# Paired residue tails, slot sums from ScalarE, wide early slot outputs and a new order of stores in an attention and mixture-of-experts kernel

## The chip, the cores and the metric

The kernel runs on one core of a Trainium2 chip. The metric is the device time in microseconds (us) of that core. The six executions of the kernel before beside the changed one lie within 0.3% of their median (181.59 to 182.62 us around 182.07); some executions of other kernels are slower by more (order4: two of 185.53 and 187.42 us, two of 198.23 and 199.43) and are called slow. Each run lists the core's span and the mean granted clock of TensorE (1.0 is full speed; the clock records of the traces of before and after hold 1.0 and 0.5 alone). The median of the kernel before was 182.08 us (182.07 to 182.35) when the prediction was made.

## The reference, cut to what matters

```python
# attention: batch 8, heads 8, sequence 576, head size 64
# heads 0-3: rel = i - j in [0, 32)        (the "plain" heads)
# heads 4-7: rel in [0, 128), rel % 4 == 0 (the "dilated" heads)
x = softmax(mask(q @ k.T / 8)) @ v              # x: 4608 tokens x 512
# soft mixture of experts: 8 experts, 4 slots each, hidden size 1024
logits = x @ phi                                # 4608 x 32
d = softmax(logits, axis=0)                     # over the tokens, for each slot
slot_input = d.T @ x                            # 32 x 512
slot_out[e] = relu(slot_input[e] @ w1[e]) @ w2[e]
out = softmax(logits, axis=1) @ slot_out        # 4608 x 512
```

Nothing can be stored before all of the attention is done, because a slot sums over all tokens; and no output column before all of w1 and that column of every w2 have been read. The loads are converted from f32 to f16 on the way, the stores from f16 to f32 (on the page of the kernel before, 61.93 MB are read from HBM and 9.44 MB written).

## The kernel before

A dilated head is four interleaved sequences ("residues") of 144 tokens. A product of this kernel takes 128 of them (128*128 in the lines of the trace), so each residue leaves a tail of 16. These are the scores and the products with v as the kernel before has them:

```python
# scores, second group of a batch (g == 1): four narrow products a head for the tails
for r in range(DIL):                               # DIL = 4
    w = LEFT if r < 3 else 2 * LEFT                # LEFT = 16
    jobs.append((kd, SUB * r + 96, qd, SUB * r + 128, W1 + LEFT * r, w))
...
# emit_av, last group of the dilated heads: 128-column products, then the tails
elif t < DIL:
    jobs.append((0, 128, n, pt[:, h % 2, 128 * t : 128 * t + 128], vD[...]))
else:
    for r in range(DIL):                           # 48 rows x 32 columns of the array
        c0 = W1 + LEFT * r
        jobs.append((32 * r, 32, n, pt[0:48, h % 2, c0 : c0 + 32], vL[b % NV][0:48, h, r, 0 : D + 1]))
...
# back_u: slot inputs, and a product with ones that sums the exponentials
for c in range(2):
    jobs.append((c, x[:, c, :], er[0:n, t, :]))
jobs.append((4, ones[0:n, :], er[0:n, t, :]))
```

After the last batch it forms the slot outputs in two halves of 256 columns, and stores 16 of the 36 blocks of 128 tokens as left halves while the right halves of two experts are still loading.

The softmax here doesn't subtract the row's maximum and nothing guards it: scores larger than these inputs give would overflow.

## Time and profile before

| | before |
|---|---|
| median time | 182.08 us |
| profiled span, mean clock | 181.0 us, 0.868 |
| one batch of attention at full clock | 13.67 us |
| last slot-input product ends | 136.77 us |
| first store issued | 152.88 us |

Second, two batches late in the attention (windows of the same trace; the last three columns are granted clock, DMA share and GB/s).

```profile
84.87:98.54 13.67, 13.45 (x271) 8.52 (x270) 10.47 (x23) 9.19 (x16) 6.32 (x9) 1.00 1.17 209
98.54:112.21 13.67, 13.46 (x272) 8.51 (x271) 10.49 (x23) 9.19 (x16) 5.88 (x8) 1.00 1.16 210
```

A window here runs from the first bias product of a batch to that of the next. At full clock a batch is 13.67 us, and TensorE is busy for 13.45 of them: it is the engine that paces the attention.

### The profile page before, as it was taken

Reading aid. Unit: us, or ns where it says so; the run is one execution under the profiler, and the core shown is the slowest. Engines: PE = TensorE matmul, PEld = TensorE weight load, DVE = VectorE, ACT = ScalarE, POOL = GpSimd, SP = SyncE. Lnnn points to the kernel's source line nnn. Section 1 sums busy time; section 2 is a strip of 40 time slices with the busy share of each in tenths; the row PEclk is TensorE's granted clock in tenths of the full one; section 3 lists DMA queues with packets and bytes.
Section 4 is the critical chain, followed back from the end, with each engine's and each line's share of the span. In section 5 each row is a group of like instructions: output and inputs, shape, how many; then the busy total and the mean of one; then the engine's idle time right before and its main releaser. Section 6 shows DMA issues by size and latency. Waiting matters only on the chain.

```text
span 181.0 us, 5591 instructions
## 1 busy us (share of the span) xinstructions
PE 146.4 (81%) x2464; PEld 87.4 (48%) x2464; DVE 107.5 (59%) x232; ACT 91.0 (50%) x162; POOL 83.9 (46%) x124
## 2 busy tenths in 40 slices
PE   0467977999999999999999999999987986598000
PEld 0133544746755665664674674675735363233000
DVE  4689874875757676588498498453604023389030
ACT  2044454748465484755766776675430024488030
POOL 7953552642623263352544327434410442979900
PEclk9999995798589789789999999999855699879855
DMA  4999999999999999999999999999999999999996
GB/s 60 199 196 208 208 210 214 201 211 214 202 212 214 203 212 214 201 211 213 203 214 211 204 216 210 214 215 215 211 216 213 200 193 163 311 332 409 410 404 239
DMA packets 29527, 40.75 MB, mean 225 GB/s; under 512 B 1856, under 2 KB 19264, under 8 KB 29504
## 3 DMA queue, kind: packets, MB, share of 16 engines
q0 software_dynamic: 28960, 39.36, 116.3%
q1 hardware_dynamic: 544, 1.05, 1.5%
q8 instruction: 19, 0.31, 0.6%
q14 instruction: 4, 0.03, 0.0%
HBM read 61.93 MB, written 9.44 MB: 394 GB/s over the span
## 4 chain that ended last, share of the span: by engine, by line
DMA 43%; PE 34%; ACT 6%; DVE 6%; POOL 5%; issue 3%; POOLq 0%; DVEq 0%
DMA w<-in_moe_w_dram 28%; DMA raw<-in_k_dram 9%; ACT p L293 5%; PE lg L408 5%; PE o_p L339 4%; PE sa L282 4%; DMA out_dram<-ol 4%; PE sb L271 4%; PE sa L271 4%; DMA out_dram<-ot 2%; PE rd L389 2%; DVE qk L245 2%; PE vb L163 2%; PE va L163 2%; PE u L452 2%
## 5 line engine op out<-in xcount | busy, mean ns | idle before, releaser
L293 ACT ACTIVATE p<-sa 128x960 f16<-128x960 f32 (+2 forms) x24 | 21.4, 891 | 33.9 <-PE sb L282 33.4
L339 PEld LDWEIGHTS <-p 128*128 128x128 f16 (+2 forms) x544 | 19.7, 99 | 12.8 <-issue 8.6
L245 DVE STREAM_TRANSPOSE qk<-raw 128x320 uint32<-128x320 uint32 (+1 forms) x32 | 21.6, 678 | 0.3
L271 PE MATMUL sa<-masks,ident 128*128 128x480 f16 (+2 forms) x48 | 15.6, 414 | 7.3 <-POOL masks L489 6.2
L293 ACT ACTIVATE p<-sb 128x960 f16<-128x960 f32 (+2 forms) x24 | 21.2, 884 | 0.0
L236 DVE STREAM_TRANSPOSE qk<-raw 128x576 uint32<-128x576 uint32 x16 | 19.8, 1249 | 0.9 <-DMA raw<-in_q_dram 0.8
L271 PEld LDWEIGHTS <-ident 128*128 128x128 f16 x96 | 9.6, 112 | 18.9 <-issue 7.7
L282 PEld LDWEIGHTS <-qk 32*128 32x128 f16 x832 | 12.6, 100 | 12.0 <-issue 9.8
L408 PE MATMUL lg<-xTd,phi 128*128 128x288 f16 x32 | 18.3, 659 | 0.0
L339 PE MATMUL o_p<-v,p 128*128 128x65 f16 (+1 forms) x288 | 16.6, 202 | 0.8 <-ACT v L172 0.7
L282 PE MATMUL sa<-qk 32*128 32x160 f16 (+4 forms) x416 | 16.5, 217 | 0.8 <-DVE qk L236 0.7
L282 PE MATMUL sb<-qk 32*128 32x160 f16 (+4 forms) x416 | 16.5, 218 | 0.0
L271 PE MATMUL sb<-masks,ident 128*128 128x480 f16 (+2 forms) x48 | 15.4, 411 | 0.5 <-ACT p L293 0.5
L209 POOL COPY v<-v 32x1024 f16<-32x1024 f16 x8 | 8.3, 1036 | 16.1 <-PE sb L282 9.4
L212 POOL DMA_DIRECT2D w<-in_moe_w_dram x16 | 8.9, 554 | 14.4 <-DMA vs<-in_v_dram 6.8
L361 DVE TENSOR_TENSOR xp<-o_p,rc_p 128x448 f16<-128x448 f32 (+1 forms) x24 | 14.4, 602 | 0.8
L361 DVE TENSOR_TENSOR xd<-o_d,rc_d 128x448 f16<-128x448 f32 (+1 forms) x24 | 14.4, 602 | 0.8
L219 POOL DMA_DIRECT2D w<-in_moe_w_dram x10 | 6.7, 673 | 14.5 <-DMA w<-in_moe_w_dram 10.2
L163 PE MATMUL va<-vs,orders 32*128 32x256 f16 (+1 forms) x96 | 12.1, 289 | 1.0 <-ACT p L293 1.0
L412 ACT ACTIVATE ET<-lg 128x288 f16<-128x288 f32 x16 | 6.6, 411 | 12.3 <-PE lg L408 12.1
L360 DVE RECIPROCAL rc_p<-o_p 128x7 f32<-128x7 f32 (+1 forms) x24 | 4.8, 198 | 12.1 <-PE o_p L339 11.6
L382 ACT COPY xTp<-rp 128x576 f16<-128x576 f16 x16 | 10.4, 647 | 2.2 <-PE rp L377 2.2
(108 smaller groups left out, 277.9 us busy)
## 6 DMA issues: line engine op xcount, KB each, us to landing
w<-in_moe_w_dram POOLq DMA_DIRECT2D x16, 512.0 KB, 16.8
w<-in_moe_w_dram POOLq DMA_DIRECT2D x5, 1024.0 KB, 19.3
vs<-in_v_dram POOLq DMA_DIRECT2D x8, 512.0 KB, 14.5
raw<-in_q_dram POOLq DMA_DIRECT2D x7, 576.0 KB, 16.6
raw<-in_k_dram POOLq DMA_DIRECT2D x7, 576.0 KB, 16.8
out_dram<-ot POOLq DMA_DIRECT2D x14, 256.0 KB, 4.2
out_dram<-of POOLq DMA_DIRECT2D x7, 512.0 KB, 4.9
w<-in_moe_w_dram POOLq DMA_DIRECT2D x8, 256.0 KB, 10.2
```

What stands on the lines that cost most here:

```text
L163: nc.tensor.matmul(o.rearrange("p (h d) -> p h d", h=4), l, st[:, 0:4, D * r : D * r + D], start=(r == 0), stop=(r == DIL - 1), skip_group ...
L209: nc.gpsimd.tensor_copy(out=vL[b % NV][0:32, :, :, 0:D], in_=vD[b % NV][96:128, :, :, 0:D])
L212: nc.gpsimd.dma_start(out=w1t[e][:, 2 * i : 2 * i + 2, :].rearrange("p l f -> p (l f)"), in_=moe_w1[e, 256 * i : 256 * i + 256].rearrange( ...
L236: nc.vector.transpose(out=dst, in_=src)
L245: nc.vector.transpose(out=o, in_=i)
L271: nc.tensor.matmul(sps[h // 2][:, h % 2, 0:n], ident, bias[g], start=True, stop=False, skip_group_check=True,)
L282: nc.tensor.matmul(sps[h // 2][:, h % 2, c0 : c0 + w], kt_[32 * h : 32 * h + 32, k0 : k0 + 128, tt], qt_[32 * h : 32 * h + 32, q0 : q0 + w ...
L293: nc.scalar.activation(out=pt, in_=sps[ab][:, :, 0:n], func=AF.Exp, scale=SCALE)
L339: nc.tensor.matmul(o[p0 : p0 + np_, n, :], l, rr, start=(k == 0), stop=(k == len(jobs) - 1), skip_group_check=True,)
L361: nc.vector.tensor_tensor(out=x.rearrange("p t (h d) -> p (t h) d", h=4)[0:nq, u0:u1, :], in0=o[0:nq, 0:n, 0:D], in1=rc[0:nq, 0:n, None].b ...
L382: nc.scalar.copy(out=xTp_t[b][:, c, :], in_=rg)
L408: nc.tensor.matmul(lp, phi4[:, kc].rearrange("p c s -> p (c s)"), rhs, start=(kc == 0), stop=(kc == 3))
```

## The change

The intent: fewer and larger products for the tails (two residues in one), no products with ones, early slot outputs 512 columns wide, 20 left-half blocks instead of 16 to cover the last loads, stores four blocks at a time with four tokens a row, and rows of 4 KB. The core of the diff:

```diff
-NLEFT = 5 * LEFT
+NLEFT = DIL * LEFT
-NSPLIT = 16
+NSPLIT = 20
@@ emit_scores (the left keys are gathered by a new copy on VectorE)
-                for r in range(DIL):
-                    w = LEFT if r < 3 else 2 * LEFT
-                    jobs.append((kd, SUB * r + 96, qd, SUB * r + 128, W1 + LEFT * r, w))
+                for u in range(2):
+                    jobs.append((kL[b % 2], 128 * u, None, 0, W1 + NLEFT * u, NLEFT))
+                    if qt_ is None:
+                        qq = qd[heads, 0:S, tt].rearrange("p (r i) -> p i r", r=DIL)[:, 128:SUB]
@@ emit_av
-                for r in range(DIL):
-                    c0 = W1 + LEFT * r
-                    jobs.append((32 * r, 32, n, pt[0:48, ...], vL[b % NV][0:48, h, r, 0 : D + 1]))
+                for u in range(2):
+                    c1 = W1 + NLEFT * (u + 1)
+                    m = (128, 64)[u]
+                    jobs.append((128 - m, m, n, pt[:, h % 2, c1 - m : c1], vL[b % NV][:, h, u, 0 : D + 1]))
@@ back_xT_dil (fifth transpose)
+            p0 = 0 if r < DIL else NLEFT
+                xd_t[b][p0:128, r, 128 * c : 128 * c + 128], ident[p0:128, p0:128],
@@ back_logits, back_u
+            accum_out=esum[:, 2 * b + half : 2 * b + half + 1],
-            jobs.append((4, ones[0:n, :], er[0:n, t, :]))
@@ prologue, on VectorE before the first transposes of q and k
+        nc.vector.tensor_scalar(out=masks[:, W1:], in0=masks[:, W1:], scalar1=gap, scalar2=None, op0=ALU.max)
@@ weights, slot outputs, stores
+    LATE_ROWS = {MIXED: ((4, 8),), 6: ((0, 8),), 7: ((0, 4), (4, 8))}
+        slot_out(so_early, 0, early, True, True)
+        nc.scalar.copy(out=early_sb, in_=so_early)
+        return out[t0 : t0 + 512].rearrange("(p k) n -> p k n", k=4)[:, blk % 4 : blk % 4 + n]
... (allocations, masks, copies of v, order of the stores and buffers cut)
```

## The prediction

> **What bounds the kernel now.** I read the page first, for the shape of the whole span.
>
> ```profile
> PE   0467977999999999999999999999987986598000
> DMA  4999999999999999999999999999999999999996
> GB/s 60 199 196 208 208 210 214 201 211 214 202 212 214 203 212 214 201 211 213 203 214 211 204 216 210 214 215 215 211 216 213 200 193 163 311 332 409 410 404 239
> ```
>
> The DMA row is full from the first slice to the last. Loads halve their bytes on the way (f32 to f16), so 210 GB/s written is about 420 read; stores do the opposite and reach 409. The kernel is one DMA stream of 30.9 MB written by loads, then 9.44 MB of stores. What can be won is where the rate falls between (slices of 163, 311, 332), and what can be lost is a store that comes late. Next I cut that stretch into windows of 1 us (the last two columns are DMA share and GB/s).
>
> ```profile
> 151.00:152.00 1.00, 0.49 (x6) 0.38 (x6) 0.00 (x0) 0.37 (x1) 0.00 (x0) 1.00 1.40 188
> 152.00:153.00 1.00, 0.98 (x10) 0.72 (x9) 0.71 (x2) 0.82 (x2) 0.12 (x1) 1.00 0.93 125
> 153.00:154.00 1.00, 0.81 (x13) 0.28 (x10) 1.00 (x3) 1.00 (x4) 1.00 (x3) 1.00 0.73 107
> 154.00:155.00 1.00, 0.68 (x12) 0.40 (x5) 0.85 (x2) 0.73 (x3) 1.00 (x2) 1.00 1.37 246
> 160.00:161.00 1.00, 1.00 (x5) 0.49 (x4) 0.89 (x2) 0.88 (x3) 0.86 (x2) 0.80 0.70 136
> 166.00:167.00 1.00, 0.89 (x6) 0.38 (x4) 1.00 (x3) 1.00 (x3) 1.00 (x2) 1.00 1.52 406
> ```
>
> Two holes: 152 to 156, where some DMA engines have finished their share of the last loads and no store is queued, and 160 to 161, where the left-half stores are through and the first full-width store is not yet issued. By packet sizes, 0.28 MB of loads (1.4 us at 195 GB/s) and 2.47 MB of stores (6.0 us at 409) moved between 152 and 162: 7.5 us of work in 10, so 2.5 us were lost. The time line tells why.
>
> ```profile
> 146.54 3.38 PE L722 MATMUL so<-w,hTm 128*32 128x256 f16 x104 [0.38 <-DVE hTm L703]
> 151.04 0.29 PE L722 MATMUL so<-w,hTm 128*32 128x256 f16 x4 [1.11 <-DMA w<-in_moe_w_dram]
> 152.88 1.09 POOL L746 DMA_DIRECT2D out_dram<-oo  x2 [5.80 <-DVE oo L743]
> 153.96 5.01 POOL L784 DMA_DIRECT2D out_dram<-ot  x7
> 159.82 2.43 POOL L814 DMA_DIRECT2D out_dram<-of  x3 [0.84 <-ACT of L803]
> ```
>
> The last left half of w2 lands at 151.0, the first store is issued 1.9 us later and its packets flow from 154.0. Seven stores of 256 KB take 5.01 us to issue, 0.72 each, while the transfer needs 0.64: issue-bound. And TensorE waits for the left half only 1.11 us. That is all the slack the compute chain has; before it, TensorE is busy 13.46 of 13.67 us of a batch (window 96.00 to 109.67, clock 1.00).
>
> [...]
>
> ```profile
> 100.46 0.28 PE L422 MATMUL ep<-ident,ET 32*128 32x32 f16 x4
> 100.68 0.21 PE L428 MATMUL ep<-ident,ET 32*32 32x32 f16 x4
> 100.82 0.39 PE L339 MATMUL o_d<-v,p 128*128 128x65 f16 x7
> 101.04 0.52 PE L377 MATMUL rp<-ident,xp 128*128 128x128 f16 x5
> 103.08 0.47 PE L339 MATMUL o_d<-v,p 128*128 128x65 f16 x18
> 103.48 0.53 PE L377 MATMUL rp<-ident,xp 128*128 128x128 f16 x5
> ```
>
> Seven o_d matmuls of one mode take 0.22 us from start to start of the next group (0.03 each), but four transposes that start at 100.68 hold the next mode back until 100.82 though they start within 0.01 of each other. In every change of mode that I looked up in this batch the start-to-start time is 0.11 to 0.13 instead of 0.03: about 0.09 us a change. [...] of the logits' matmuls of 288 columns, those that read xTd with a stride occupy 18.3 us in 32, those that read xTp in order 7.2; start to start it is 0.48 against 0.125 us, 1.66 ns a column against 0.43. [...] here the fill rate is the same 405 to 413 for 1 KB and 2 KB store packets, so I expect nothing from rows of 4 KB.
>
> **The change, part by part.**
> 1. Stores. 20 blocks instead of 16 leave as left halves, so they cover 2.62 MB / 0.409 = 6.4 us instead of 5.1. By fours a store is 512 KB (1.28 us of transfer) for one issue; loads with four pieces per partition issue in 0.75, so the issue bound goes: about 0.35 us.
> 2. Loads. Right halves of 2.5 experts are 1.31 MB instead of 1.05: the last left half lands 1.3 us earlier, near 149.7. A quarter MB more on either side goes in 512-byte packets (197 GB/s instead of 214): +0.2 us.
> 3. Wide early outputs. 96 early matmuls of 256 columns become 44 of 512. In fours, 24 groups of 0.107 become 11 of 0.216: 2.4 us for about 2.7, less the copy to SBUF (0.69 for 512 columns on ScalarE), part of which is then waited for. About nothing, if TensorE is in time.
> 4. Paired tails and slot sums, per batch, on TensorE. Attention times v: 16 small matmuls in one mode (18 with two others: 0.40 us to the next group) become 8 that alternate between 128x128 and 128x64, which the built program confirms: 8 changes instead of 2. Two at 0.03, seven intervals and an exit of 0.12: 1.02 us, +0.62. Transposes of xd: the fifth now has 64 rows, so four more changes, 0.36, less 0.06 for shorter ones: +0.30. Row transposes: three fewer and one change fewer, -0.10. The ones matmuls: five fewer at 0.025, -0.13 (the two changes there stay). Bias: 48 columns more, four times 0.02, +0.08. Scores: 8 groups of four that took 0.24 become 4 of 64 strided columns, 4 x 0.106 = 0.42: +0.18, if row tiles pay the stride as full ones do. Sum +0.95 us a batch, 7.6 in eight.
> 5. Start. VectorE now waits for GpSimd's masks before its first transposes (six more selects or so, 0.2 to 0.3 each): +1.3 us, of which batch 1's wait for its data may hide half. Take +0.6.
> 6. Extra gathers on VectorE (7.5 to 10.5 busy of 13.67) and copies on GpSimd lie beside TensorE: nothing.
>
> Parts 4 and 5 lie on TensorE's path to the early outputs: about 8 us. The DMA queue doesn't feel it until the end, as issues lead landings by some 14 us. But the slack is 1.1.
>
> **The sum.** With no delay of TensorE, so_sb would be ready at about 150.4 (149.7 plus matmuls, the copy and the sum) and the first store issued near 151.6, flowing near 152.6. With a delay d that is 152.6 + d. For small d: the first hole shrinks by 1.2, the issue bound goes (0.35), the second hole shrinks by perhaps 0.3, +0.2 for loads: about 180.5. For large d all loads are in, nothing else interrupts, and the stores take 9.44/0.409 = 23.1 plus 0.4 of starting bubbles; 0.9 to the last landing and 1.0 to the end as before, and runs are 1.1 above the profiled span. So time = 152.6 + d + 26.5 = 179.1 + d, true for d above about 3. d = 8 gives 187.1.
>
> **Rivals.** (a) TensorE is not delayed: changes of mode to 128x64 are cheap, or the granted clock, half for 20 us of the first 80 here, happens to stay full [...]. Then only the holes count: 180.5. For it: the sizes (20 blocks, 2.5 experts) fit exactly the two holes, as if fitted by measurement. Against: six added changes and four more in the transposes, all with measured counterparts. (b) A half delay, d = 3 to 6, because the strided reads or the start cost nothing: 182 to 185. (c) The clock gets worse: batches of 13.67 us at full clock may lose their step when they grow to 14.6, and stretches at half clock come back: d = 10, 189. I lean to the delay, since each of its terms is read off this trace, and shade it for (a) and (b).
>
> **Range and chances.** 30% for about 180.5, 70% for a delay with a middle of 7 to 8. The point between is 185.5; 180.0 to 189.0 should hold it 8 times in 10. Slower by over 2% means above 185.7: 0.49. Faster by over 2% means below 178.4, which needs both holes closed and more: 0.04. Within 2%: 0.47.
>
> **What would show it.** After: the last slot transposes and u matmuls some 8 us later than 136.7; the first store at about 160 instead of 152.9, with the DMA rate near zero from 156 and then 409 without a second hole; the eight o_d tail matmuls spread over about 1 us; xd transposes with 0.1 us steps. If instead TensorE still waits for the last left half and the first store is issued before 153, the delay is wrong and rival (a) holds. If a batch at full clock is no longer than 13.7 us, part 4 is wrong.

## More of the kernel before

The prediction shows the DMA rows of the page and the stretch in which loads give way to stores. Two more views matter for what follows. First, from the page of the kernel before: TensorE's busy share, the granted clock in tenths over the 40 slices of the span, and the chain that ended last.

```profile
PE 146.4 (81%) x2464; PEld 87.4 (48%) x2464; DVE 107.5 (59%) x232; ACT 91.0 (50%) x162; POOL 83.9 (46%) x124
...
PEclk9999995798589789789999999999855699879855
...
DMA 43%; PE 34%; ACT 6%; DVE 6%; POOL 5%; issue 3%; POOLq 0%; DVEq 0%
```

The reader should see that the clock drops to half now and then in the first half of this profiled execution (5s, 7s and 8s), and that the largest share of the chain is DMA (43%, TensorE 34%): what TensorE loses there may hide behind the loads.

## The result, and the profile after

The changed kernel took 195.2 us (median of 6, 193.95 to 197.64, the last one slow), against 182.07 us (181.59 to 182.62) for the kernel before in the same rounds. The ratio is 1.071 (95% interval 1.067 to 1.076): slower, and outside the predicted range of 180 to 189. A ratio is the mean time of one kernel's fast runs over that of the other's of the same rounds, so it is not quite the ratio of the medians.

The page of the changed kernel, rows over 40 slices of 4.84 us and the chain that ended last:

```profile
PE   0366987999999999999999999999997888885000
...
PEclk9999997579999799957978999997985579999755
DMA  4999999999999999999997999999999970899993
GB/s 73 194 204 204 214 208 212 206 210 208 209 210 206 211 214 202 212 215 198 203 213 92 209 225 218 212 215 193 203 181 184 197 106 0 166 403 408 414 406 159
...
DMA 8%; PE 7%; DVE 2%; ACT 2%; issue 1%; DVEq 0%; POOLq 0%; ACTq 0%
```

The DMA row now has a gap: slice 33 moves nothing at all. It also has a dip at slice 21 (92 GB/s; slices are counted from 0), where loads were issued late: GpSimd, which issues them, issued none between 95.0 and 102.4 us, as the copy before them waited 4.9 us for VectorE. The chain is cut short (its shares add up to 20%), so the time line has to tell what the stores waited for. The columns are start, duration, engine, line, operation, output and input, count, and in brackets the idle time before it and what ended it.

```profile
149.93 0.43 PE L472 MATMUL u<-er,xp 128*128 128x32 f16 x10 [0.42 <-DVE er L456]
150.19 0.54 PE L472 MATMUL u<-er,xd 128*128 128x32 f16 x10
152.80 0.23 DVE L717 TENSOR_TENSOR siTm<-UT,rcol 128x128 f16<-128x128 f32 x1
153.08 5.73 PE L731 MATMUL hps<-w,siTm 128*32 128x512 f16 x64 [0.62 <-DVE siTm L717]
160.62 2.59 PE L783 MATMUL so_early<-w,hTm 128*32 128x512 f16 x44
163.04 0.72 PE L783 MATMUL so<-w,hTm 128*32 128x256 f16 x20
163.26 0.59 ACT L880 COPY early_sb<-so_early 128x512 f32<-128x512 f32 x1 [2.02 <-PE so_early L783]
163.88 0.42 DVE L795 TENSOR_TENSOR so_sb<-early_sb,so 128x256 f16<-128x256 f32 x1 [3.07 <-ACT early_sb L880]
165.49 1.11 POOL L809 DMA_DIRECT2D out_dram<-oo  x2 [18.14 <-DVE oo L806]
```

The last slot-input products (u) end at 150.73 instead of 136.77 us: 14.0 us late. None of the late slot outputs (so) waits for a load any more. The first store is issued at 165.49 instead of 152.88, 12.6 us later, and the profiled span is 12.5 us longer (193.5 against 181.0). From the first store to the end both kernels take 28.1 us. So the whole loss lies before the first store.

Where the attention got longer, four batches of the changed kernel show (windows as above):

```profile
58.96:74.93 15.97, 15.64 (x239) 9.44 (x238) 10.92 (x24) 9.62 (x18) 6.34 (x10) 0.89 1.16 209
74.93:92.45 17.52, 17.20 (x240) 10.13 (x239) 10.92 (x24) 9.77 (x18) 6.34 (x10) 0.81 1.21 208
92.45:108.63 16.18, 15.85 (x240) 9.54 (x239) 10.93 (x24) 9.73 (x18) 8.26 (x14) 0.89 1.02 173
108.63:123.61 14.98, 14.65 (x240) 8.96 (x239) 11.23 (x24) 9.62 (x18) 4.46 (x8) 1.00 1.05 216
```

Two losses are to be told apart. At full clock a batch takes 14.98 us, 1.31 more than before. And most batches are not at full clock: with a mean of 0.81, 19% is missing, so about 38% of 17.52 us, 6.7 us, ran at half clock, and that batch is 2.5 us longer than 14.98. In the clock records, every half-clock stretch that ends within the record is a multiple of 3.41 us (in the changed kernel's trace 10.24, 3.41, 6.83, 3.41, 3.41 and 13.65 us).

Within a batch at full clock, the largest single difference is the last group of the dilated outputs, two products of 128 columns and the eight tails. From its start to the start of the next group (transposes, rp) in the changed kernel:

```profile
113.17 1.26 PE L352 MATMUL o_d<-v,p 128*128 128x65 f16 x10
114.36 0.53 PE L390 MATMUL rp<-ident,xp 128*128 128x128 f16 x5
```

1.19 us, where the kernel before needs 0.40 (103.08 to 103.48 in the prediction). Start to start, a 128-column product is followed by a 64-column one after 134 ns, and that by a 128-column one after 150 ns; two of the same shape follow after 29 ns.

### The profile page after: what moved, and what is told of

Same layout as the page of the kernel before. It is cut to its first block, busy times and chain, and to the rows that moved or that the text cites. A ratio compares the mean times of both kernels' runs of the same rounds, so it can differ in the third digit from the quotient of the medians.

```text
span 193.5 us, 5050 instructions
## 1 busy us (share of the span) xinstructions
PE 156.6 (81%) x2170; PEld 92.1 (48%) x2170; DVE 111.9 (58%) x253; ACT 94.2 (49%) x179; POOL 80.3 (41%) x137
## 5 line engine op out<-in xcount | busy, mean ns | idle before, releaser
L352 PEld LDWEIGHTS <-p 128*128 128x128 f16 (+1 forms) x480 | 25.3, 104 | 16.3 <-issue 10.2
L216 POOL COPY v<-v 32x512 f16<-32x512 f16 x16 | 9.8, 611 | 33.2 <-DVE v L206 27.9
L286 PE MATMUL sa<-masks,ident 128*128 128x480 f16 (+2 forms) x48 | 16.4, 432 | 7.3 <-POOL masks L525 6.2
L352 PE MATMUL o_p<-v,p 128*128 128x65 f16 (+1 forms) x288 | 18.0, 212 | 0.7 <-ACT v L176 0.7
L302 PEld LDWEIGHTS <-qk 32*128 32x128 f16 x576 | 11.1, 105 | 14.4 <-issue 10.9
L302 PE MATMUL sa<-qk 32*128 32x160 f16 (+2 forms) x288 | 15.5, 249 | 2.2 <-DVE qk L245 2.2
L286 PE MATMUL sb<-masks,ident 128*128 128x480 f16 (+2 forms) x48 | 16.6, 437 | 0.1
L352 PE MATMUL o_d<-v,p 128*128 128x65 f16 x192 | 16.3, 201 | 0.0
L302 PE MATMUL sb<-qk 32*128 32x160 f16 (+2 forms) x288 | 15.5, 249 | 0.0
L374 DVE TENSOR_TENSOR xp<-o_p,rc_p 128x448 f16<-128x448 f32 (+1 forms) x24 | 14.4, 602 | 0.8
L221 POOL DMA_DIRECT2D w<-in_moe_w_dram x16 | 8.9, 558 | 6.7 <-DMA vs<-in_v_dram 3.0
```

The source lines that it names most:

```text
L216: nc.gpsimd.tensor_copy(out=vL[b % NV][64 * w : 64 * w + 32, :, :, 0:D], in_=high[:, :, :, w, 0:D])
L221: nc.gpsimd.dma_start(out=w1t[e][:, 2 * i : 2 * i + 2, :].rearrange("p l f -> p (l f)"), in_=moe_w1[e, 256 * i : 256 * i + 256].rearrange( ...
L286: nc.tensor.matmul(sps[h // 2][:, h % 2, 0:n], ident, bias[g], start=True, stop=False, skip_group_check=True,)
L302: nc.tensor.matmul(sps[h // 2][:, h % 2, c0 : c0 + w], kt_[heads, k0 : k0 + 128, tt], qq, start=False, stop=(jn == len(jobs) - 1 and tt == 1),
L352: nc.tensor.matmul(o[p0 : p0 + np_, n, :], l, rr, start=(k == 0), stop=(k == len(jobs) - 1), skip_group_check=True,)
L374: nc.vector.tensor_tensor(out=x.rearrange("p t (h d) -> p (t h) d", h=4)[0:nq, u0:u1, :], in0=o[0:nq, 0:n, 0:D], in1=rc[0:nq, 0:n, None].b ...
```

## The experiments

Twelve kernels ran. All gave correct results, and the kernel before ran beside them on the same chip each time (the first four on chip 9, the next four on chip 4, the last four on chip 7); the changed kernel itself was not run again. The first four split the change.

**attn: the changed attention with the loads, slot outputs and stores of before.**

```diff
+ the hunks emit_scores, emit_av, back_xT_dil, back_logits, back_u and prologue of the change
  NSPLIT = 16, HALVED = (6, 7): loads of w2, slot outputs and stores as before
```

> The reverse: the changed kernel's attention (paired tails, slot sums from ScalarE) with the old loads, early outputs and stores. T: 194 to 197 us, as the end of the attention sets the first store and the DMA tail has nothing to win back. D: near 182 to 184 us.

Measured: 193.65 us (193.21 to 195.08), ratio 1.064 (1.059 to 1.070), mean clock 0.854 to 0.864. The loss lies in the attention.

**tail: the other half of the change on the attention of before.**

```diff
-NSPLIT = 16
+NSPLIT = 20
+ the hunks for the loads of w2, the slot outputs and the stores
  attention, row transposes and slot sums as before
```

> The kernel before with the changed kernel's loads, wide early outputs and stores (20 left blocks by fours, 2.5 experts last, four-token rows), and the old attention with its small tails and ones matmuls. Theory T (the added time is all TensorE's in the attention, through the first store): the delay goes, the first store is issued before 153 us, the holes in the DMA stream shrink: 180 to 181.5 us. Rival D (the new loads, packets or stores themselves cost): above 188 us.

Measured: 182.18 us (181.59 to 183.36), ratio 1.001 (0.995 to 1.006). It costs nothing, but it doesn't gain the 1 to 2 us either. The DMA row of its page has no slice below the rate of the late loads until the stores run out:

```profile
GB/s 63 196 197 211 204 211 212 204 211 213 203 213 214 202 213 212 204 212 211 206 212 210 210 209 217 216 220 210 213 220 205 192 196 190 353 406 409 409 380 177
```

The holes of before are gone; its first store is issued at 151.44 instead of 152.88, and its span is 179.9 us. But spans of the kernel before in the same rounds were 179.8 to 181.0, so the holes were worth less than the 2.5 us that the prediction counted.

**m128: the changed kernel without the alternation of shapes.** The 64-column product of a pair is widened to 128; the extra columns fill output rows that nothing reads.

```diff
-                    m = (128, 64)[u]
+                    m = 128
```

> The changed kernel with the second tail matmul of a head over all 128 output rows, as the first is: same values where they are read, no change of tiling mode in attention times v. T: TensorE's 8 changes a batch, which cost 1.18 us from the first tail to the next group against 0.40 before, fall to about 0.33: 0.8 us a batch, so 6 us less, 189 us. D: no change, 195 us. Rival C (the granted clock alone): no change beyond 1 to 2 us unless the half-clock stretches move.

Measured: 182.71 us (181.97 to 183.32), ratio 1.003 (0.997 to 1.008). One word wins back 12.5 us, all of the loss; the theory expected 6. The batch at full clock is 14.10 us, 0.88 less, and the group that took 1.19 us takes 0.31:

```profile
117.23 0.48 PE L352 MATMUL o_d<-v,p 128*128 128x65 f16 x10
117.54 0.52 PE L390 MATMUL rp<-ident,xp 128*128 128x128 f16 x5
```

But 8 x 0.88 is 7.0 us. The last u product ended 14.4 us earlier than in the changed kernel (136.31 against 150.73). The rest came with the clock, whose mean was 0.891 to 0.910 in its four runs instead of 0.846 to 0.863.

**rd128: the changed kernel with its fifth transpose at full 128 rows**, which removes four other changes of shape.

```diff
-            p0 = 0 if r < DIL else NLEFT
             nc.tensor.transpose(
-                rg[:, 128 * r : 128 * r + 128 - p0],
-                xd_t[b][p0:128, r, 128 * c : 128 * c + 128],
-                ident[p0:128, p0:128],
+                rg[:, 128 * r : 128 * r + 128], xd_t[b][:, r, 128 * c : 128 * c + 128], ident
             )
```

> The changed kernel with the fifth transpose of xd over all 128 rows again, in the mode of the four others. T: four changes of mode a batch fewer, 0.31 us a batch, 2.5 us in all: 192.7 us. D: 195 us. C: as for m128.

Measured: 190.49 us for its only fast run, at clock 0.876; three others, called slow, took 194.8 to 198.5 at 0.823 to 0.844. The batch at full clock is 14.67 us, so the 0.31 us are real (2.5 us in eight batches). On the time it is inconclusive: the clock swings by more than the effect.

The second group asks why m128 won twice what its products cost.

**order: the same eight tails, the four wide ones first.** Same work, 2 changes of shape instead of 8.

```diff
                     m = (128, 64)[u]
-                    jobs.append((128 - m, m, n, pt[:, h % 2, c1 - m : c1], vL[b % NV][:, h, u, 0 : D + 1]))
+                    (jobs if u == 0 else over).append(
+                        (128 - m, m, n, pt[:, h % 2, c1 - m : c1], vL[b % NV][:, h, u, 0 : D + 1])
+                    )
```

> The changed kernel with the eight residue-tail products of a batch in another order: first the four of 128 columns (u = 0, one for each head), then the four of 64 columns (u = 1), so that the array changes its shape 2 times a batch there instead of 8. The work, its data and its widths are the same. Theory C (each change of shape costs TensorE about 0.11 us, as the batch of 14.98 us at full clock in the changed kernel and 14.10 us with all eight tails at 128 columns suggest: 0.88 us for 8 changes): the batch falls by 6 x 0.11 = 0.66 to about 14.3 us, the last u product ends near 138 us instead of 150.7, and the time is 183 to 185 us. Rival W (it is the 64-column product itself or its place in the rows 64 to 127 that is dear, not the alternation): the batch stays within 0.2 us of 14.98 and the time above 191 us. As to the clock: if the lower mean clock of the changed kernel (0.85 to 0.86, against 0.89 to 0.91 with the tails at 128) comes with the changes of shape, it is back at 0.885 or more here; if it comes with something else, it stays below 0.87.

Measured: batch 14.33 us at full clock, and the group in the trace:

```profile
120.44 0.60 PE L354 MATMUL o_d<-v,p 128*128 128x65 f16 x10
120.97 0.53 PE L392 MATMUL rp<-ident,xp 128*128 128x128 f16 x5
```

0.53 us: six changes fewer save 0.66 us, 0.11 each. The last u product ended at 139.96, two us after the 138 expected, as some early batches ran partly at half clock. Its two fast runs took 181.87 and 183.77 us (ratio 1.004, 0.999 to 1.009), two slow ones 185.6 and 186.9; clock 0.891 to 0.926 in all four. Theory C holds in the batch and in the clock. The 64-column product is not dear in itself; rival W falls.

**pad: no alternation, but dense work of the same length instead.**

```diff
-                    m = (128, 64)[u]
+                    m = 128
-        for h in range(4):
+        for h in range(4) if g else (0, 1, 2, 3, 0, 1, 2, 3):
             nc.tensor.matmul(sps[h // 2][:, h % 2, 0:n], ident, bias[g], ...)
```

> The changed kernel with all tails at 128 columns (no alternation) and TensorE made longer by dense work instead: the four bias products of the first score group are issued twice (the second overwrites the first with the same values). 4 x 480 columns are about 0.80 us a batch at full clock, near the 0.88 us that the alternation cost. It tells apart how much of the 12.5 us is time on TensorE as such, and how much a lower clock that belongs to the changes of shape. Theory L (length alone, the clock stays at 0.89 or above): batch 14.9 us at full clock, the last u product ends near 136.3 + 6.4 = 143 us, some 1.5 us of it hidden by the loads, time 186 to 189 us. Theory K (the clock falls with the length or density of TensorE's work, whatever the shapes): mean clock 0.87 or below and 191 us or more. If the extra work is wholly hidden, 183 us, which would contradict both.

Measured: 184.32 us (184.06 to 184.87), ratio 1.013 (1.010 to 1.015), clock 0.903 to 0.942. Three batches of it:

```profile
56.59:71.50 14.91, 14.59 (x244) 8.80 (x242) 10.74 (x24) 9.53 (x18) 6.33 (x10) 1.00 1.16 209
71.50:86.41 14.91, 14.58 (x244) 8.80 (x243) 10.75 (x24) 9.53 (x18) 6.33 (x10) 1.00 1.16 210
86.41:101.32 14.91, 14.59 (x244) 8.80 (x242) 10.73 (x24) 9.53 (x18) 7.21 (x12) 1.00 1.16 210
```

This is the run that bounds the two parts of the loss. A batch here is as long as in the changed kernel (14.91 against 14.98 at full clock), and the time is 184.3, not 195.2. It beat the 186 to 189 of theory L as well, for two reasons. Its last u product came at 140.58, not at 143, as its clock was better: 3.4 us at half clock before that product, where m128's profiled execution had 9.0 and the changed kernel's 34.3. And more than half of the 4.3 us by which it came after m128's (136.31) was hidden by the loads that m128 still had in flight. At the same length, then, the changed kernel takes nearly 11 us more (195.2 less 184.3), and that is about the most that the lower clock can be worth. It is not the clock's exact share of the 12.5: pad takes only 1.6 us more than m128 (1.8 by the ratios, as they ran in different rounds, on different chips), but with a better clock than m128 had. If no part of the 7.0 us of length were hidden, 5.5 us would be left for the clock.

**all4: the changed kernel with four repairs** (m128, rd128, the left scores' queries read along memory with a strided write to PSUM, and VectorE's last step on the masks after the first two transposes).

```diff
-                        qq = qd[heads, 0:S, tt].rearrange("p (r i) -> p i r", r=DIL)[:, 128:SUB]
+                        qq = qd[heads, 0:S, tt].rearrange("p (r i) -> p r i", r=DIL)[:, :, 128:SUB]
+                    oo = sps[h // 2][:, h % 2, c0 : c0 + w]
+                    if qt_ is None:
+                        oo = oo.rearrange("p (i r) -> p r i", r=DIL)
... (m128, rd128 as above; masks' step moved two lines down)
```

> The changed kernel with four repairs of its attention: all tails at 128 columns, the fifth transpose of the dilated halves at full 128 rows, the left scores read their queries along memory and write PSUM with a stride, and the masks' last step on VectorE after the first two transposes of the queries and keys instead of before them. If the losses found so far add up (0.88 + 0.31 + about 0.3 us a batch, and part of the 2.4 us of the start), the batch is 13.5 to 13.7 us, as short as before's 13.67. Theory F (the loads and stores are the floor, about 180 us of span: then a shorter attention gains nothing any more): 181.0 to 182.3 us, ratio 0.990 to 1.002, the same as the kernel before. Rival: TensorE still held m128 back, so 179.5 to 181 us, clearly faster than before.

Measured: 181.95 us (181.67 to 182.12), ratio 0.999 (0.997 to 1.001). The batch is 13.56 us, shorter than before's. From the time line of its trace, the late slot outputs (so) before the first store:

```profile
145.62 0.28 PE L783 MATMUL so<-w,hTm 128*32 128x256 f16 x4
...
146.76 0.40 PE L783 MATMUL so<-w,hTm 128*32 128x256 f16 x8 [0.86 <-DMA w<-in_moe_w_dram]
148.10 0.29 PE L783 MATMUL so<-w,hTm 128*32 128x256 f16 x4 [0.94 <-DMA w<-in_moe_w_dram]
149.44 0.29 PE L783 MATMUL so<-w,hTm 128*32 128x256 f16 x4 [1.05 <-DMA w<-in_moe_w_dram]
```

TensorE waits for the loads again, three times about 1 us. Theory F holds: repaired, the attention is off the path, and the kernel meets a floor of loads and stores.

**tail_sums: before's scores and tails with the changed kernel's tail end and ScalarE slot sums.**

```diff
  tail, and:
+            accum_out=esum[:, 2 * b + half : 2 * b + half + 1],
-            jobs.append((4, ones[0:n, :], er[0:n, t, :]))
-        nc.vector.tensor_tensor(out=er, in0=ep, in1=emask, op=ALU.mult)
+        nc.vector.tensor_copy(out=er, in_=ep)
```

> The kernel before's scores and tails (four tails of 32 columns a head), with the changed kernel's tail end and its slot sums from ACT (accumulating exponentials, no ones products on TensorE, no mask multiply). The ones products were worth 0.13 us a batch on TensorE and their removal shortens it to about 13.5 us; ACT pays 16 x 0.19 us off the path. Theory F (loads and stores are the floor): 181 to 182.3 us, the same as before and as the tail end alone (182.18). Rival: 180 to 181 us, faster.

Measured: 182.44 us (181.46 to 182.75), ratio 1.001 (0.999 to 1.004). It has the shortest batch of all (13.35 us) and its last u product at 131.07 us, 5.7 us before that of the kernel before, and gains nothing: the floor again.

The third group asks whether the clock follows the alternation elsewhere, and by degrees.

**before_alt: the kernel before with 8 more changes of shape a batch.** Products of 128 and 32 columns in the last group of the plain outputs alternate instead of standing one kind after the other.

```diff
+        if kind == "p" and i == 2:
+            mix = []
+            for k, x in enumerate(jobs):
+                mix.append(x)
+                if k < 4:
+                    mix.append(over[k])
+            jobs, over = mix, over[4:]
         jobs += over
```

> The kernel before with nothing but the order of 12 products of a batch changed: in the last group of the plain outputs the products of 128 columns and those of 32 columns alternate for four pairs, which makes 8 changes of shape a batch more. Same work, same results. Length alone: 8 x about 0.11 us, so a batch of about 14.5 us at full clock instead of 13.67; the last u product some 7 us later than the 133 to 137 us of the kernel before, of which 1.5 to 3 us hide behind the loads. Theory S (changes of shape [...] pull the granted clock down, as order and pad suggest): mean clock 0.87 or below, 188 to 194 us. Rival Q (the low clock belonged to something else in the changed attention, such as products on 64 of the array's columns): mean clock 0.885 or above, and 183 to 187 us.

Measured: a batch of 14.51 us, as expected from 0.11 us a change; the twelve products now stretch over 1.49 us:

```profile
115.82 1.49 PE L346 MATMUL o_p<-v,p 128*128 128x65 f16 x12
```

The only fast run took 185.83 us at clock 0.874; three slow ones took 189.2 to 193.1 at 0.846 to 0.860. The clock of all four lies low among those of the kernel before on the same chip (0.869 to 0.910), but the fast run's time fits rival Q's range and its clock lies between the two. The cost in length is confirmed in a second place. About the clock this run leaves the matter open, since only its slow runs show the large loss.

**order4: the tails by pairs of heads, 4 changes of shape.**

```diff
+                if h % 2:
+                    jobs[-3], jobs[-2] = jobs[-2], jobs[-3]
```

> The changed kernel with the eight tail products ordered by pairs of heads (128, 128, 64, 64, twice): 4 changes of shape a batch instead of 8 in the changed kernel and 2 in order. Length alone: 14.98 - 4 x 0.11 = 14.54 us a batch at full clock. If the clock follows the number of changes step by step, its mean lies between the 0.85 to 0.86 of 8 changes and the 0.89 to 0.93 of 2, near 0.875, and the time between 184.7 and 195.2 us, 187 to 191. If there is a threshold, it is like the one or the other: clock 0.89 or above and 184 to 187 us, or 0.86 and 192 us or more.

Measured: batch 14.54 us, to the digit. Two fast runs of 185.53 and 187.42 us at clock 0.899 and 0.883, two slow ones of 198.2 and 199.4 at 0.828 and 0.822. It is neither a steady middle nor one of the ends: the same kernel is found in two regimes.

The last two ask what the clock answers to.

**after_pad: the changed kernel, alternation kept, with pad's dense work on top.** Its edit is that of pad alone.

> The changed kernel with its eight changes of shape kept, and with the four bias products of the first score group issued twice, as in pad: 0.80 us of dense work a batch ON TOP of the slow tails. It asks what the lower granted clock answers to. Theory A (activity[...]): the clock comes back to 0.88 or more, the batch is 14.98 + 0.80 = 15.8 us at full clock, the last u product ends near 148 us, and the time is 191 to 195 us, no slower than the changed kernel although it does more. Theory S (the changes of shape themselves bring the low clock, whatever lies around them): the clock stays at 0.865 or less, and the time is the changed kernel's plus 6 us or more, 200 us and up.

Measured: 203.22 us for the fast run at clock 0.819, three slow ones of 208.7 to 209.3 at 0.790 to 0.808. From its page, which shows one of the slow runs (209.16 us):

```profile
PEclk9999995599699669857975995599785559999855
```

Theory A's forecast failed: the added work did not bring the clock back. Even in the fast run it was lower than in every run of the changed kernel (0.846 to 0.863), while the same work without the alternation ran at 0.90 to 0.94. But this work stands at the start of a batch, 4 to 5 us before the tails, so it doesn't fill the stretch in which they stand. What the traces show of that stretch comes under "Why the prediction was wrong".

**thin: no alternation, the batch lengthened by 32 products of 2 columns.**

```diff
+        for i in range(32 if g == 0 else 0):
+            c0 = 8 * (i // 4)
+            nc.tensor.matmul(sps[i % 4 // 2][:, i % 2, c0 : c0 + 2], ident, masks[:, c0 : c0 + 2], start=True, ...)
         for h in range(4):
... (m = 128 as in m128)
```

> The changed kernel with all tails at 128 columns (no alternation) and the batch made longer as in pad, but by 32 products of 2 columns instead of 4 of 480: about 26 ns each from start to start (as the products of 1 column in the kernel before), 0.83 us a batch in which the array streams next to nothing. The values are overwritten by the bias products that follow. Theory A (activity): the clock falls as under the alternation, mean 0.87 or less, and the time is 189 us or more although there is not one change of shape more than in m128. Theory S (changes of shape): the clock stays at 0.89 or more as in pad, and the time is that of pad, 183.5 to 185.5 us.

Measured: batch 14.90 us; fast runs of 185.51 and 188.23 us at clock 0.928 and 0.903, slow ones of 189.4 and 191.0 at 0.930 and 0.887. The ratio, 1.040, fits the mean of the last three runs, two of them slow; the two fast ones give 1.025. The clock is that of theory S. The time is not: its median of 188.81 is above S's range, and one slow run was at 0.930. What these runs lost besides the clock is not known, as only the first one left a trace (span 183.8 us). These products, too, stand at the start of a batch and not at the tails.

## Why the prediction was wrong

The prediction was 185.5 us, and 195.2 was measured. Between its delayed case, 187.1, and 195.2 lie 8.1 us: d was 14.0 instead of 8, and the formula 2.1 short. Against the profile of before, the 6.0 of d are 2.9 of part 4, 1.8 of part 5 and about 1 of clock. Its steps, in order:

- **"The kernel is one DMA stream" with 1.11 us of slack on TensorE, and a delay that goes straight to the end: right.** The first store was to be issued at 151.6 + d; with d = 14.0 that is 165.6, and it was 165.49. Its place in the time line, the empty DMA row before it and the absence of a second hole came as described.
- **The formula 179.1 + d: right in form, 2.1 us short.** For d = 14.0 it gives 193.1. The store rate needed longer to rise than the 0.4 us counted. In windows of 1 us after the first store of the changed kernel it was

```profile
166.00:167.00 1.00, 0.85 (x8) 0.58 (x6) 1.00 (x3) 1.00 (x4) 1.00 (x3) 1.00 0.63 129
167.00:168.00 1.00, 1.00 (x18) 0.51 (x20) 0.80 (x3) 1.00 (x3) 1.00 (x3) 1.00 0.86 174
168.00:169.00 1.00, 0.44 (x10) 0.16 (x10) 0.88 (x2) 0.87 (x3) 1.00 (x3) 1.00 1.79 367
```

  in GB/s (last column), which against 409 is 557 KB, or 1.4 us, lost. Another 0.6 us is that runs are 1.7, not 1.1, above the profiled span.
- **Part 4, "+0.95 us a batch": this step failed in size.** It measured 1.31. Tails: 0.79 instead of 0.62, as a change to 64 columns and back takes 134 and 150 ns, not 120. One term was missing: ScalarE's exponential of the second score group grew from 608 to 704 columns, 0.677 to 0.757 us each, and TensorE waits 0.11 us longer for it before the reorder of v. The other terms were nearly right: transposes of xd +0.36 instead of +0.30 (rd128 won back 0.31 of it), strided scores +0.21 instead of +0.18, bias +0.09, row transposes -0.11, ones products -0.14. The strided scores came out by luck: their last group holds the next mode back for 0.214 us, not the 0.106 counted, and the groups before took 0.33 us to the next mode, not 0.24. In eight batches: 10.5 us instead of 7.6.
- **Part 5, the start: 2.4 us later by the second batch instead of 0.6** (24.35 against 21.92). Part of this is scatter: with the set-up of before, the second batch starts at 21.92 to 23.56 in four traces (before, tail, tail_sums, before_alt), with the changed one at 23.72 to 24.38 in nine. Moving the masks' step in all4 brought the second score group back to where it was before (10.69 us; before 10.75, changed kernel 12.21), but the second batch only to 23.78. No run isolates what is lost in between.
- **The clock: named as rival (c) and then left out of d; this step failed too.** Against the profile that the prediction used, the clock seems to explain little: 10.5 + 2.4 of the 14.0 us are length and start. But that execution of before had itself 27.6 us at half clock before its last u product (the changed one 34.3). The experiments ask the better question, what the changed kernel would take without the alternation: 182.7, with 9.0 us at half clock and the last u product 14.4 us earlier. Of these 14.4 us, 7.0 are the length of the alternation, and 7.4 the clock and what else changed. Of the 12.5 us of time, the clock's share lies between 5.5 and nearly 11 (see pad). Rival (c) had the direction, but gave the clock 2 us (a d of 10 instead of 8). Its reason, that batches lose their step when they grow, falls with pad, whose batches of 14.91 us ran at full clock.
- **"Nothing from rows of 4 KB": right.** In the settled part of the stores, 409 GB/s in the changed kernel (175 to 190 us) and 407 in the kernel before (163 to 179 us).
- **Parts 1 to 3, the tail end: harmless as predicted, but without the gain.** Rival (a) gave 180.5 for an undelayed TensorE; tail took 182.18 and all4 181.95. The step that failed is "2.5 us were lost" in the two holes as time to be had: with them closed, the time stayed within 0.3 us.

What is shown: the alternation of 128 and 64 columns is the cause of the loss (attn, m128, order), a change of shape costs 0.11 us (order, order4, before_alt), and the mean clock is lower in every run of the changed kernel and of attn (0.846 to 0.864) than in every run of that attention without it (m128, pad and, with more repairs, all4: 0.888 to 0.942). A low mean alone costs nothing: the kernel before took 182.44 us at 0.859. As far as the traces show, half clock costs time where it falls into the attention and uses up the slack (before the last u product the changed kernel had 34.3 us of it, m128 9.0; its share of the 12.5 us of time lies between 5.5 and nearly 11). What no experiment shows is why the clock falls. Idle time of TensorE does not account for it: in the batch with clock 0.81 it was busy for 17.20 of 17.52 us. Nor does little work in the array at just any place of a batch: thin left the array nearly empty for about as long in each batch (14.90 us against 14.10 in m128) as the alternation lasts (0.88 us) and kept its clock (0.887 to 0.930), and dense work added to the alternation did not bring it back (after_pad, 0.790 to 0.819). With fewer changes (order4) or elsewhere (before_alt), executions of one kernel fall on either side.

Both thin and after_pad put their products 4 to 5 us before the tails, and the kept traces show that the place matters. Cut each trace along the 3.41 us steps of its clock record (every stretch that ends within it is a whole number of them). Give each matmul the columns that it streams, times the part of the 128x128 array that its operands cover (256 columns on 16 rows and 64 columns of the array count as 16), and add up what starts in a step. From 18 us to the last u product, 392 steps of the 14 traces (those of before_alt and after_pad are of slow runs) ran at full clock. The 57 that were followed by half clock hold 1,152 to 3,056 such columns, the 335 that were followed by full clock 2,542 to 6,302; a cut at 2,850, fitted to these same steps, sorts all but 12. These are the steps in which the group with the tails begins, for the six times that it follows a reorder of v:

| | columns in the step, in order of time | next step at half clock |
|---|---|---|
| after | 3112, 2184, 2792, 2376, 3464, 2344 | second, third, fourth and sixth |
| m128 | 4170, 3594, 3500, 3329, 3272, 4401 | none |
| after_pad | 2248, 2568, 2533, 2440, 2541, 2376 | all |
| thin | 3503, 4369, 4170, 3337, 3962, 3594 | none |

So the traces point to theory A in a narrower form: half clock goes with little work of the array within one step, and the alternation thins out a step that is thin already, as the reorder of v before it uses 16 to 32 rows (32*128 and 16*64 in the trace). It might also explain the two regimes of one kernel, if the steps fall differently against the batches from one execution to the next; that was not shown. This is a correlation. No run put dense work beside the tails, which would test it, so the cause of the low clock stays open.

## What to carry to other kernels

Order products so that those of one array shape stand together, and widen a narrow one with columns that nothing reads rather than alternate: here two products of 128 columns, each of them half waste, took 58 ns, and 284 ns with one of the two at 64 columns. When an edit lengthens the engine that paces a stage, look at the granted clock of that stage in both traces before summing durations: here 7.0 us of changes of shape came with a last product that was 14.4 us later. And before shortening a stage, ask what else sets the end: five kernels with batches from 13.35 to 14.10 us (before, tail, m128, all4, tail_sums) ended within 0.8 us of each other, because loads and stores fill the span (on the page of the kernel before, 38 of 40 slices have a DMA share of 90% or more).

## More costs that the traces show

- A change of shape took 0.11 us on average: 134 ns from 128x128 to 128x64 and 150 ns back, against 29 ns between products of one shape; 8 changes a batch were 0.88 us.
- Half clock came with TensorE 98% busy (17.20 of 17.52 us, clock 0.81) when shapes alternated, and with added dense work it fell to 0.79 to 0.82; without the alternation it was 0.89 to 0.94. The columns weighted by the part of the array in use told the steps apart (a cut at 2,850 sorts all but 12 of 392), while TensorE's busy time did not: 15 of the 57 steps before half clock were over 95% busy.
- For the left scores (four products of 64 columns, start to start) a strided moving operand took 0.107 us, 1.67 ns a column; the same with the stride on PSUM's side took 0.055 us, 0.86 ns a column (0.03 us without a stride, in the 64-column scores of the plain heads). So PSUM was the cheaper place for the stride here.
- Batching the stores into rows of 4 KB gained nothing: 407 GB/s with rows of 1 and 2 KB, 409 with rows of 4 KB among those of 1 KB.
- An accumulating exponential on ScalarE was followed by a read of the accumulator of 194 ns (16 of them, 3.1 us, off the path).
